# Reordering VectorE between neighbouring steps of an FFT convolution that shares one core with a gated MLP

## The chip, the cores and the metric

The kernel runs on one core of a Trainium2 chip. The metric is device time in microseconds (us) for one execution, and the time of a version is the median of its runs. The engines are named as in the profile: PE (TensorE), DVE (VectorE), ACT (ScalarE), POOL (GpSimd) and SP (SyncE, which here only issues transfers).

## The reference, cut to what matters

The input is normalised, goes through two branches, and the three are summed.

```python
def _A_ref(u, log_A_real, A_imag, C_real, C_imag, log_dt, D_skip):
    ...                                   # A, C from the parameters; P = exp(A dt pos)
    K = 2.0 * jnp.einsum("dn,dnl->dl", C, P).real       # D x L kernel, N = 256 terms
    Kf = jnp.fft.rfft(K, 2 * L)
    Uf = jnp.fft.rfft(u_t, 2 * L)
    y = jnp.fft.irfft(Uf * Kf[None, :, :], 2 * L)[:, :, :L]
    ...
    return y + u * D_skip[None, None, :]

def _B_ref(x, w_gate, w_up, w_down):
    h = _sigmoid(x @ w_gate) * (x @ w_up)
    return h @ w_down

xn = _layernorm(A_u)
return A_u + _A_ref(xn, ...) + _B_ref(xn, ...)
```

L = 2048 positions, D = 448 channels, N = 256 state terms, F = 1792 hidden units; everything is float32.

## The kernel before, in words

Two Python generators, `conv()` and `glu()`, write the instructions of the two branches. Each hands back an estimated cost at every `yield`; the loop at the end of the kernel always advances the one whose `done / total` is smaller. So the order in which the matmuls of both branches are written is a matter of these numbers alone: `total[0]` holds, among others, 17 times `WS` = 7.0 for the 17 steps described below. Tile then schedules the written instructions onto the engines' queues at build time: an instruction that is ready goes ahead of one that is not, a lower place in the text goes first, `hp(HP)` moves an instruction 300 places forward, and `tc.issue_after(x)` puts the instructions of a block behind x where both are on the same engine. On the chip every queue is worked through in that order.

**The MLP (`glu`).** It goes in two halves of 1024 tokens (two tiles of 512), and in each half over 14 slices f of 128 hidden units in groups of three (or two). For a slice and a token tile there are two *gate halves* of 11 matmuls each (gate and up projections, L710; float32 is made of a high and a low part, three products). ACT and DVE make `th`, `hf` (L721), `hh` and `hl` (L728) out of them. After a group come eight *down chunks* of 9 matmuls (6 in the group of two; L824), each added to `acc` by DVE (L829). In the second half the slices 4, 5, 0, 1 and 2 load raw weights through POOL's DMA queue and POOL itself splits them into high and low part (`wh` L772, `wl` L773, `dh` L798, `dl` L799); the raw gate/up weights and the raw down weights of these slices use one buffer, `wraw`, in turn. At the second chunk of the last group `glu` yields `None`: it is then held until `conv` is through.

**The convolution (`conv`).** A long part (`kgen`) generates K and its first transform stage until about 557 us. Then `spectra` makes the second stage of both transforms, the product, and the way back, in 17 *steps* (h, k): eight with h = 0 (channels 0 to 223), one for k = 32, eight with h = 1. The list `ks` gives the order of k. One step is:

- `there` (L892 to L926): 32 matmuls into the PSUM tile `pk` (from K) and 32 into `px` (from the input; L908). For each of the two, ACT copies the odd part to `oo` (L912), and DVE forms sum and difference of even part and `oo` (L914, L915), which are written to the tiles `kk` and `xx`. These four DVE instructions are called *the reading* (the "forward sums" of the change) here, since they free `pk` and `px`. Then come two products on DVE (`yy`, L919, and `kk` in place, L920), two combinations on POOL (L921 on `yy`; L922, which reads `kk` and writes `yy`), and DVE's *sum and difference* `sd` of the two halves of `yy` (L924, L925).
- `back` (L928 to L957): 32 matmuls of `sd` (L937) into the same two PSUM tiles `pk` and `px`, ACT's copies to `vt` (L943), and stores from `vt` to the DRAM tensor `v_d` (two transfers; six for k = 0).

`kk`, `xx` and `yy` have one buffer each, `sd` and `oo` two. The loop writes `there(n)`, then (after half a step's cost) `back(n-1)`, and so on. The input tiles of a step are loaded three steps ahead. PE's order is fixed: the list `sp_mm` holds the latest matmul and `issue_after` puts the next spectra block behind the MLP's matmuls that were written before it, and the other way round.

When two steps k and k+16 are through, `turned` loads their rows of `v_d` back as `vp` (SP's queue). When all of h = 0 is there, `last(0, q)` (L965 to L986) does the last stage for the quarters q = 0 to 3 of the positions: 64 matmuls (L973) into `pk` (even q) or `px` (odd q), which DVE adds to `ac` or `acc` (L982). In the loop two quarters are written together after one step, the other two together after the next. For h = 1, `last(1, q)` is written within the MLP's last group, after its fifth down chunk.

Of the kernel before, what the change touches and what calls it, by code (L numbers as in the profile page):

```python
# [15 lines left out]
ALU = mybir.AluOpType  # L16
# [12 lines left out]
NFT = F // 128  # L29
WK = 5.5  # L30
WS = 7.0
HOLE = 6
AHEAD = 46
WP = 5
WX = 2
HELD = 9
LATE = 3.6
HP = 300
Y0 = (8, 1)
# [13 lines left out]
NCK = D // DC  # L53
# [74 lines left out]
def s4d_glu_kernel(ctx, tc, io):  # L128
    nc = tc.nc
    hp = tc.high_priority  # L130
    v = nc.vector
# [106 lines left out]
    def out_end(src, b0, ds, engs=(nc.sync, nc.scalar)):  # L238
        for g in range(4):
            to = blocks(out_t, g, b0, src.shape[1])  # L240
            engs[g % len(engs)].dma_start(to[:, :, ds], src[32 * g : 32 * g + 32, :, ds])
# [606 lines left out]
    def spectra(pf):  # L848
# [16 lines left out]
        def work(n, sh, bufs):  # L865
            return spare[n].pop() if spare.get(n) else pf.tile(sh, F32, name=n, bufs=bufs)
# [22 lines left out]
        def after():  # L889
            return tc.issue_after(sp_mm[0].ins)  # L890

        def there(k, tb, sk, sx):  # L892

            n = 2 if k == 32 else 4
            np_ = 32 * n
            both = []
            for j, src in enumerate((sk, sx)):
                with after():
                    for c in range(2):
                        for g in range(n):  # L900
                            for p in range(2):
                                s = slice(64 * p, 64 * p + 64)
                                to = pb[j][32 * g : 32 * g + 32, p, H * c : H * c + H]
                                rhs = sx[s, g]
                                if src is sk:
                                    to, rhs = to.rearrange("p (g d) -> p g d", d=32), sk[s, :, g]
                                w = (t32[s, 0] if k == 32 else tb[s, g])[:, 32 * c : 32 * c + 32]
                                mm = nc.tensor.matmul(to, w, rhs, start=True, stop=True, skip_group_check=True)  # L908
                sp_mm[:] = [mm]
                ev, od = (half(pb[j][:np_, p, : 2 * H]) for p in range(2))  # L910
                oo = work("oo", [128, 2, H], 2)
                nc.scalar.copy(oo[:np_], od)  # L912
                t = work(("kk", "xx")[j], [128, 2, 2, H], 1)
                v.tensor_tensor(t[:np_, 0], ev, oo[:np_], ALU.add)  # L914
                v.tensor_tensor(t[:np_, 1], ev, oo[:np_], ALU.subtract)  # L915
                both.append(t[:np_])
            kk, xx = both
            yy = work("yy", [128, 2, 2, H], 1)[:np_]
            v.tensor_tensor(yy, kk, xx, ALU.mult)  # L919
            v.tensor_tensor(kk, kk, xx[:, :, ::-1], ALU.mult)  # L920
            nc.gpsimd.tensor_tensor(yy[:, :, 0], yy[:, :, 0], yy[:, :, 1], ALU.subtract)  # L921
            nc.gpsimd.tensor_tensor(yy[:, :, 1], kk[:, :, 0], kk[:, :, 1], ALU.add)  # L922
            sd = work("sd", [128, 2, 2, H], 2)
            v.tensor_tensor(sd[:np_, 0], yy[:, 0], yy[:, 1], ALU.add)  # L924
            v.tensor_tensor(sd[:np_, 1], yy[:, 0], yy[:, 1], ALU.subtract)  # L925
            return sd  # L926

        def back(h, k, sd, engs=(nc.sync, nc.sync)):  # L928
            vt = work("vt", [128, 4, H], 2)
            n = 2 if k == 32 else 4  # L930
            bt = t32[:, 1:].rearrange("p (q e) m -> p q e m", q=2) if k == 32 else bk
            with after():
                for e in range(2):
                    for g in range(n):
                        s = slice(32 * g, 32 * g + 32)
                        for p in range(2):
                            mm = nc.tensor.matmul(  # L937
                                pb[g // 2][64 * p : 64 * p + 64, g % 2, :H], bt[s, p, e], sd[s, p, e],
                                start=(e == 0), stop=(e == 1), skip_group_check=True,
                            )  # L940
            sp_mm[:] = [mm]
            for j in range(n // 2):
                nc.scalar.copy(vt[:, 2 * j : 2 * j + 2], pb[j][:, :, :H])  # L943

            for p in range(2):
                s = slice(64 * p, 64 * p + 64)
                real = slice(64 * p, 64 * p + 64, 2)
                to = lambda h_: v_d[h_, s].rearrange("(c g q) w d -> w c g q d", c=2, g=4)
                if k == 32:
                    for j in range(2):  # L950
                        engs[p].dma_start(to(j)[:, 1, 0, 0], vt[real, j])
                elif k == 0:
                    engs[p].dma_start(to(h)[:, 0, 0, 0], vt[real, 0])
                    for c in range(2):
                        engs[p].dma_start(to(h)[:, c, 1:, 0], vt[64 * p + c : 64 * p + 64 : 2, 1:])
                else:
                    engs[p].dma_start(to(h)[:, :, :, k // 4], vt[s])  # L957
# [7 lines left out]
        def last(h, q):  # L965

            for p in range(2):
                s = slice(64 * p, 64 * p + 64)
                for i in range(2):
                    for g in range(4):  # L970
                        w = 16 * (q % 2) + 4 * g + 2 * (q // 2) + i
                        with after():
                            mm = nc.tensor.matmul(  # L973
                                pb[q % 2][32 * g : 32 * g + 32, p, H * i : H * i + H], wf[s, w], vp[h][s, w],
                                start=True, stop=True, skip_group_check=True,
                            )
            sp_mm[:] = [mm]
            ds = slice(H * h, H * h + H)
            acc = ac[:, 4 * q : 4 * q + 4] if q < 2 else accs[q]
            for p in range(2):  # L980
                a = acc[:, p::2, ds]
                v.tensor_tensor(a, a, half(pb[q % 2][:, p, : 2 * H]), ALU.add)  # L982
            if h == 1 and q < 3:
                out_end(acc, 4 * q, ds, *([[nc.gpsimd]] if q == 0 else []))
            elif h == 0 and q < 2:
                out(acc, 4 * q, h)  # L986
# [2 lines left out]
        lasts.append(last)  # L989
        nc.sync.dma_start(t32, io["c_t32"])  # L990
        nc.gpsimd.dma_start(bk, io["c_bk"])
        ks = [4, 20, 0, 16, 8, 24, 12, 28]
        steps = [(0, k) for k in ks] + [(1, k) for k in ks[-NTB:] + ks[:-NTB]]
        steps[1:1] = [(None, 32)]
        tabs = {}
        ld = [loads(*s) for s in steps[:NLD]]
        nc.gpsimd.dma_start(wf, io["c_wf"])
        prev, wait, due = None, [], []
        for n, (h, k) in enumerate(steps):

            sp_mm[:] = glu_mm
            cur = there(k, *ld[n])
            if (h, k) == (0, ks[-NTB - 1]):
                for k_ in ks[:-NTB]:
                    tabs.pop(k_)
            if n + NLD < len(steps):
                ld.append(loads(*steps[n + NLD]))
            glu_on[:] = [1]
            yield WS / 2
            sp_mm[:] = glu_mm  # L1010
            if prev is not None:
                back(*prev)
            if 4 <= n < 8:
                o = slice(2 * n - 8, 2 * n - 6)
                nc.sync.dma_start(ac[:, o], acc_d[:, o])
            if prev is not None and prev[1] < 32:
                wait.append(prev[:2])

            while len(wait) > 2 and not (due and wait[0][0] == 1):
                t, u = wait.pop(0), wait.pop(0)  # L1020
                turned(*t, 4)
                if u == (0, 28):
                    due = [n + 1]
            prev = (h, k, cur)
            if n == 11:
                total[1] -= LATE
            yield WS / 2
            if due and n >= due[0]:
                sp_mm[:] = glu_mm
                for q in (0, 1, 2, 3)[2 * (n - due[0]) : 2 * (n - due[0]) + 2]:  # L1030
                    last(0, q)
                if n == due[0] + 1:
                    due = []
        sp_mm[:] = glu_mm
        back(*prev, (nc.sync, nc.scalar))
        for t in (*wait, prev[:2]):
            turned(*t)

    def conv():
# [87 lines left out]
        with tc.tile_pool(name="pf", bufs=1, side="right", reuse_waits="tile") as pf:  # L1127
            yield from spectra(pf)

    lasts, glu_mm, sp_mm, glu_on, outs, x1s, hfs, xls = [], [], [], [], [0], [0], [], []  # L1130
    xq, psc, raws, acl, marks, slots, pqs = list(x_first), [], [], [], [None, None], {}, []
    W1s, GGs, act = [], [], []
    gens = [conv(), glu()]
    total = [sum(Y0) + 11 * WP + 8 * WX + AHEAD + NCK * WK + HOLE + 17 * WS, 2 * (4 + NFT * 14.8) - HELD]
    done = [0.0, 0.0]
    done[0] += next(gens[0])
    held = False
# [38 lines left out]
```

## Time and profile before

| | |
|---|---|
| median of 3 runs | 762.92 us (757.61 to 768.84) |
| the profiled execution, its own time | 769.57 us |
| its span from first to last instruction | 767.8 us |
| mean granted TensorE clock in it | 0.945 |
| first `there` matmul of the 17 steps | 557.2 us |
| first `there` matmul of the last step | 726.0 us |

In the tables below a row of a timeline has start and duration in us, the engine, the line of the kernel, the operation with its output and inputs, how many instructions are merged into the row, and in square brackets how long the engine was idle before it and what it waited for. A row of the chain of waits has start, duration, engine, output and line. A row of the list of waits has total us, times and the longest. A row of the stage table has the stretch, its length, then busy us and instruction count of PE, PE's weight loads, DVE, ACT and POOL, the granted TensorE clock, the DMA share and GB/s. The times in the prediction are those of the profiled execution.

### The profile page before, as it was taken

The page shows a single profiled execution, that of the slowest core. Times are in us where ns is not written, and L with a number is a line of the kernel's source. Part 1 is how long each engine was busy: PE and PEld are TensorE (multiplying, and loading weights), DVE is VectorE, ACT ScalarE, POOL GpSimd, SP SyncE. Part 2 cuts the span into 40 slices and gives each one's busy share as a digit, 9 for nine tenths or more (in the row PEclk, how much of TensorE's full clock was granted, in tenths as well). Part 3 has the DMA queues.
Part 4 walks back from the last instruction along what each step waited for, and adds up shares of the span by engine and source line. Part 5 has one row for each costly group of instructions (what it writes and reads, how often), then busy time and mean ns, then how long its engine had stood idle before and what let it go on. Part 6 is the DMA issues. An engine that isn't in the chain of part 4 may idle for free.

```text
span 767.8 us, 22542 instructions
## 1 busy us (share of the span) xinstructions
PE 678.1 (88%) x9477; PEld 520.6 (68%) x9477; DVE 602.3 (78%) x777; ACT 423.1 (55%) x651; POOL 427.1 (56%) x455
## 2 busy tenths in 40 slices
PE   3897699999998988888899999899899799968966
PEld 2664588877876877555778777788667567645754
DVE  6798996789998998876659988787397567777843
ACT  3544466477787888787377777767413222212310
POOL 2110065748889889974636776754146553675211
PEclk9997989999999999798999999999999999988997
DMA  9934265345234543344744134304588757775464
GB/s 209 208 126 160 79 200 178 117 137 177 78 102 151 180 118 96 116 151 144 229 136 146 38 95 141 93 20 142 149 260 233 213 159 205 214 206 163 114 161 126
DMA packets 93462, 114.58 MB, mean 149 GB/s; under 512 B 12848, under 2 KB 83056, under 8 KB 93104
## 3 DMA queue, kind: packets, MB, share of 16 engines
q1 hardware_dynamic: 71632, 92.54, 41.1%
q10 hardware_dynamic: 19248, 14.91, 6.9%
q0 software_dynamic: 2480, 5.67, 2.8%
q8 instruction: 75, 1.23, 0.7%
q14 instruction: 27, 0.22, 0.1%
HBM read 68.32 MB, written 44.76 MB: 147 GB/s over the span
## 4 chain that ended last, share of the span: by engine, by line
PE 34%; DVE 9%; issue 4%; POOL 4%; DMA 4%; ACT 2%; SPq 1%; ACTq 0%; DVEq 0%; POOLq 0%
PE gu L710 14%; PE po L824 7%; PE ko L619 4%; PE tr L535 2%; POOL yy L921 1%; DMA v_d<-vt 1%; POOL yy L922 1%; PE pk L908 1%; DVE yy L919 1%; DVE Ft L605 1%; DVE sd L925 1%; PE kp L561 1%; PE px L908 1%; DMA wraw<-in_B_w_up_dram 1%; DMA rdw<-in_B_w_down_dram 1%
## 5 line engine op out<-in xcount | busy, mean ns | idle before, releaser
L513 POOL TENSOR_TENSOR me<-me,pm 128x32 f32<-128x32 f32 (+1 forms) x168 | 147.5, 878 | 84.3 <-DVE Et L604 69.6
L513 POOL TENSOR_TENSOR mf<-mf,pm 128x64 f32<-128x64 f32 (+1 forms) x112 | 122.7, 1095 | 6.1
L710 PE MATMUL gu<-xh,wh 128*128 128x512 f32 x336 | 107.8, 431 | 6.4 <-DVE acc L829 4.8
L710 PE MATMUL gu<-xh,wl 128*128 128x512 f32 x336 | 99.5, 404 | 0.0
L710 PE MATMUL gu<-xl,wh 128*128 128x512 f32 x336 | 98.3, 397 | 0.5 <-DVE xl L218 0.5
L824 PE MATMUL po<-dh,hh 128*128 128x448 f32 (+1 forms) x227 | 87.1, 384 | 10.0 <-DVE hf L721 3.8
L605 DVE TENSOR_TENSOR Ft<-mf,S 128x1024 f32<-128x1024 f32 x56 | 80.5, 1437 | 13.5 <-PE ko L619 4.4
L604 DVE TENSOR_TENSOR Et<-me,S 128x1024 f32<-128x1024 f32 x56 | 79.1, 1412 | 14.2 <-ACT me L526 14.2
L710 PEld LDWEIGHTS gu<-xh,wh 128*128 128x128 f32 x336 | 64.6, 203 | 30.2 <-issue 10.0
L824 PE MATMUL po<-dl,hh 128*128 128x448 f32 (+1 forms) x227 | 84.1, 370 | 0.0
L603 DVE TENSOR_TENSOR Et<-me,S 128x1024 f32<-128x1024 f32 x56 | 77.3, 1384 | 8.2 <-ACT S L546 7.9
L824 PE MATMUL po<-dh,hl 128*128 128x448 f32 (+1 forms) x227 | 82.8, 368 | 0.0
L543 ACT ACTIVATE S<-tr 128x1024 f32<-128x1024 f32 x56 | 57.7, 1031 | 43.6 <-PE tr L535 28.8
L726 ACT CAST hh<-hf 128x512 fp32r<-128x512 f32 x56 | 34.9, 623 | 78.3 <-DVE hf L721 77.7
L619 PEld LDWEIGHTS ko<-Et,Ft 128*32 128x32 f32 x3584 | 56.1, 115 | 30.3 <-DVE Ft L605 13.6
L710 PEld LDWEIGHTS gu<-xh,wl 128*128 128x128 f32 x336 | 66.0, 197 | 15.1
L619 PE MATMUL ko<-Et,Ft 128*32 128x64 f32 x3584 | 65.9, 228 | 11.5 <-DVE Ft L605 11.5
L710 PEld LDWEIGHTS gu<-xl,wh 128*128 128x128 f32 x336 | 63.7, 191 | 16.0 <-issue 1.4
L546 ACT ACTIVATE S<-S,hpi 128x1024 f32<-128x1024 f32 x56 | 65.6, 1171 | 0.0
L721 DVE SCALAR_TENSOR_TENSOR hf<-th,gu 128x512 f32<-128x512 f32 x56 | 38.1, 680 | 32.8 <-PE gu L710 26.1
L829 DVE SCALAR_TENSOR_TENSOR acc<-po,acc 128x448 f32<-128x448 f32 (+1 forms) x81 | 48.2, 608 | 18.6 <-PE po L824 18.6
L728 DVE TENSOR_TENSOR hl<-hf,hh 128x512 fp32r<-128x512 f32 x56 | 51.4, 918 | 14.3 <-ACT hh L726 14.2
(212 smaller groups left out, 1357.9 us busy)
## 6 DMA issues: line engine op xcount, KB each, us to landing
sk_d<-sk ACTq DMA_DIRECT2D x14, 512.0 KB
sx<-x_d SPq DMA_DIRECT2D x64, 112.0 KB
skl<-sk_d SPq DMA_DIRECT2D x16, 448.0 KB
vp<-v_d SPq DMA_DIRECT2D x7, 896.0 KB
v_d<-vt SPq DMA_DIRECT2D x27, 224.0 KB
wt_d<-wh SPq DMA_DIRECT2D x9, 512.0 KB
wt_d<-wl SPq DMA_DIRECT2D x9, 512.0 KB
wl<-wt_d SPq DMA_DIRECT2D x9, 512.0 KB
```

The source lines that it names most:

```text
L513: ins = nc.gpsimd.tensor_tensor(m[:, :, w + a : 2 * w : n], m[:, :, a:w:n], par(base + i).unsqueeze(2).to_broadcast([128, 4 * DC, w // n]) ...
L543: nc.scalar.activation(rows(cs), pv, AF.Abs)
L546: sins[:] = [nc.scalar.activation(cs, cs, AF.Sin, scale=-TWO_PI, bias=hpi)]
L603: v.tensor_tensor(Et[:, :, :, 32:64], two(me[:, :, 32:64]), S[:, 1::-1], ALU.mult)
L604: v.tensor_tensor(Et[:, :, :, 0:32], two(me[:, :, 0:32]), S[:, 1:3, :, ::-1], ALU.mult)
L605: fts[:] = [v.tensor_tensor(Ft, two(mf), S[:, 3:5], ALU.mult)]
L619: nc.tensor.matmul(ko[32 * j : 32 * j + 32, sl], Ft[:, cc, DC * h + 4 * q + j], Et[:, cc, DC * h + 4 * q + j], start=(k == 0), stop=(k == ...
L710: glu_mm[:] = [nc.tensor.matmul(ps, a_, b_, start=(n == 0), stop=(n == len(mm) - 1))]
L721: marks[1] = v.scalar_tensor_tensor(hf, th, 1.0, pgu[1], ALU.add, ALU.mult)
L728: v.tensor_tensor(hl, hf, hh, ALU.subtract)
L824: glu_mm[:] = [nc.tensor.matmul(po[:, ds], a_[:, bs], w_[:, ds], start=(n == 0), stop=(n == 3 * fc - 1))]
L829: v.scalar_tensor_tensor(acc[:, b, ds], po[:, ds], 0.5, acc[:, b, ds], ALU.mult, ALU.add)
```

## The change

It has four edits.

1. `there` is cut in three. It now ends with the reading and returns `kk`, `xx` and the reading's last instruction. The products and POOL's combinations become `product`, where POOL's two instructions get `hp(HP)`. The sum and difference become `halves`. The loop writes `there(n)`, then `halves` of step n-1 behind the reading of step n, then `product` of step n. So DVE's order changes from reading n, products n, sd n, reading n+1 to reading n, sd n-1, products n, reading n+1, sd n.
2. In the loop the quarters of `last(0, q)` are no longer written in pairs: after each one `conv` yields half a step's cost, so that MLP matmuls stand behind each quarter.
3. `total[0]` counts 19 instead of 17 times `WS`, for these four half steps.
4. The order of k goes from 4, 20, 0, 16, 8, 24, 12, 28 to 4, 20, 8, 24, 0, 16, 12, 28; the second half of the channels, which begins with the last four, goes from 8, 24, 12, 28, 4, 20, 0, 16 to 0, 16, 12, 28, 4, 20, 8, 24.

```diff
                 v.tensor_tensor(t[:np_, 0], ev, oo[:np_], ALU.add)
-                v.tensor_tensor(t[:np_, 1], ev, oo[:np_], ALU.subtract)
+                read = v.tensor_tensor(t[:np_, 1], ev, oo[:np_], ALU.subtract)
                 both.append(t[:np_])
-            kk, xx = both
+            return *both, read
+
+        def product(np_, kk, xx):
             yy = work("yy", [128, 2, 2, H], 1)[:np_]
             v.tensor_tensor(yy, kk, xx, ALU.mult)
             v.tensor_tensor(kk, kk, xx[:, :, ::-1], ALU.mult)
-            nc.gpsimd.tensor_tensor(yy[:, :, 0], yy[:, :, 0], yy[:, :, 1], ALU.subtract)
-            nc.gpsimd.tensor_tensor(yy[:, :, 1], kk[:, :, 0], kk[:, :, 1], ALU.add)
+            with hp(HP):
+                nc.gpsimd.tensor_tensor(yy[:, :, 0], yy[:, :, 0], yy[:, :, 1], ALU.subtract)
+                nc.gpsimd.tensor_tensor(yy[:, :, 1], kk[:, :, 0], kk[:, :, 1], ALU.add)
+            return yy
+
+        def halves(np_, yy):
             sd = work("sd", [128, 2, 2, H], 2)
...
-        ks = [4, 20, 0, 16, 8, 24, 12, 28]
+        ks = [4, 20, 8, 24, 0, 16, 12, 28]
...
-            cur = there(k, *ld[n])
+            np_ = 64 if k == 32 else 128
+            kk, xx, read = there(k, *ld[n])
+            if prev is not None:
+                with tc.issue_after(read.ins):
+                    sd = halves(*prev[2:])
+            cur = np_, product(np_, kk, xx)
...
-                back(*prev)
+                back(*prev[:2], sd)
...
                 for q in (0, 1, 2, 3)[2 * (n - due[0]) : 2 * (n - due[0]) + 2]:
+                    sp_mm[:] = glu_mm
                     last(0, q)
+                    yield WS / 2
...
-        back(*prev, (nc.sync, nc.scalar))
+        back(*prev[:2], halves(*prev[2:]), (nc.sync, nc.scalar))
...
-    total = [sum(Y0) + 11 * WP + 8 * WX + AHEAD + NCK * WK + HOLE + 17 * WS, 2 * (4 + NFT * 14.8) - HELD]
+    total = [sum(Y0) + 11 * WP + 8 * WX + AHEAD + NCK * WK + HOLE + 19 * WS, 2 * (4 + NFT * 14.8) - HELD]
```

More of the change, by code (lines that the diff above doesn't have):

```diff
@@ L1023, in spectra @@
                     due = [n + 1]
-            prev = (h, k, cur)
+            prev = (h, k, *cur)
             if n == 11:
```

## The prediction, made before the changed kernel was run

> **What bounds the kernel now.** I read the stage table first, to see where PE is not full; then who waits for whom; then one step on DVE and POOL; then the chain of waits.
>
> ```profile
> 300.00:540.00 240.00, 223.60 (x3846) 172.53 (x3841) 189.29 (x203) 175.39 (x260) 157.84 (x182) 0.95 0.39 121
> 557.00:709.00 152.00, 132.18 (x1709) 94.21 (x1708) 112.08 (x153) 37.19 (x71) 86.94 (x78) 0.92 0.74 208
> 709.00:731.00 22.00, 22.00 (x338) 15.65 (x344) 18.69 (x27) 7.97 (x15) 5.44 (x5) 1.00 0.47 127
> ```
>
> Ahead of the steps PE is busy 223.6 of 240 us. In the first 13 steps it stands still for 152 - 132.2 = 19.8 us at a granted clock of 0.92; in the last steps it is full. So PE's work sets the time, and what can be won lies in PE's waits and in its clock between 557 and 709 us. The list of PE's waits from 556 us on names them:
>
> ```profile
> PE pk L937 <- DVE kk L915: 9.9, 6, 3.0
> PE pk L973 <- DMA vp<-v_d: 5.7, 1, 5.7
> PE pk L908 <- DVE ac L982: 5.2, 1, 5.2
> PE pk L908 <- DVE acc L982: 3.3, 1, 3.3
> PE pk L937 <- DVE sd L924: 2.3, 1, 2.3
> PE pk L937 <- issue: 0.8, 1, 0.8
> ```
>
> Six times `back` waits for the reading that frees `pk`, twice `there` for the adds of a pair of quarters. Why the reading is late is seen in one step on DVE, and beside it on POOL:
>
> ```profile
> 622.07 0.62 DVE L924 TENSOR_TENSOR sd<-yy 128x448 f32<-128x448 f32 x1 [2.75 <-POOL yy L922]
> 622.62 0.62 DVE L925 TENSOR_TENSOR sd<-yy 128x448 f32<-128x448 f32 x1
> ...
> 624.52 0.69 DVE L728 TENSOR_TENSOR hl<-hf,hh 128x512 fp32r<-128x512 f32 x1 [0.69 <-ACT hh L726]
> 625.13 0.62 DVE L914 TENSOR_TENSOR kk<-pk,oo 128x448 f32<-128x448 f32 x1
> ...
> 626.72 0.61 DVE L915 TENSOR_TENSOR xx<-px,oo 128x448 f32<-128x448 f32 x1
> 627.37 1.09 DVE L919 TENSOR_TENSOR yy<-kk,xx 128x896 f32<-128x896 f32 x1
> 628.50 1.09 DVE L920 TENSOR_TENSOR kk<-kk,xx 128x896 f32<-128x896 f32 x1
> ...
> 631.87 0.62 DVE L924 TENSOR_TENSOR sd<-yy 128x448 f32<-128x448 f32 x1 [2.28 <-POOL yy L922]
> ```
>
> ```profile
> 628.61 2.00 POOL L921 TENSOR_TENSOR yy<-yy 128x448 f32<-128x448 f32 x1 [6.57 <-DVE yy L919]
> 630.69 1.15 POOL L922 TENSOR_TENSOR yy<-kk 128x448 f32<-128x448 f32 x1
> ```
>
> It is a ring through DVE and POOL, 631.87 - 622.07 = 9.8 us a turn: `sd`, the MLP's `hf` and `hl`, the reading, the products, POOL's two, `sd` again. What PE needs for a step stands in the chain of waits:
>
> ```profile
> 554.83 2.43 PE po L824 x12
> ...
> 569.51 0.99 PE pk L937 x16
> ...
> 570.62 1.10 PE px L937 x16
> 571.72 4.16 PE gu L710 x11
> ...
> 583.91 0.92 PE pk L908 x32
> 584.83 0.76 PE px L908 x32
> 585.59 2.78 PE gu L710 x11
> ```
>
> ```profile
> 683.33 1.75 PE pk L908 x32
> 685.08 1.49 PE px L908 x32
> 686.57 3.14 PE gu L710 x11
> ...
> 690.76 2.71 PE gu L710 x11
> ...
> 698.69 1.75 PE pk L908 x32
> 700.44 1.49 PE px L908 x32
> 701.94 3.94 PE gu L710 x11
> ```
>
> At full clock `there` takes 585.59 - 583.91 = 1.68, a gate half 2.7 (690.76), a matmul of a down chunk 2.43 / 12 = 0.20, and a `back` whose matmuls alternate between the banks 690.76 - (686.57 + 3.14) = 1.05. So a step with two gate halves needs 1.68 + 5.4 + 1.05, about 8.2 us on PE; where the ring takes 9.8, PE waits.
>
> **The change part by part: what goes.** (a) With the reading ahead of `sd`, `back(n-1)` no longer waits for it behind POOL: 9.9 + 0.8 = 10.7 us.
>
> (b) After each quarter MLP matmuls now stand on PE (a gate half of 2.7 or a down chunk of 9 x 0.20 = 1.8), and they cover the adds: two per quarter, of the size of L914, 0.62. These adds no longer stand behind an `sd` that waits for POOL. 5.2 + 3.3 = 8.5 us. If the cover were gone, half of it would be back.
>
> (c) After a wait PE runs slower for a while:
>
> ```profile
> 602.45 1.65 PE L710 MATMUL gu<-xh,wh 128*128 128x512 f32 x3
> 616.30 1.65 PE L710 MATMUL gu<-xh,wh 128*128 128x512 f32 x3
> 628.40 0.96 PE L710 MATMUL gu<-xh,wh 128*128 128x512 f32 x3
> ```
>
> Three matmuls in 1.65 instead of 0.96, and a whole gate half in 4.16 (571.72) instead of 2.7. Three such gate halves cost 3 x 1.4 = 4.2; the two `there` at 683.33 and 698.69 took 3.24 instead of 1.68 and the gate halves behind them 0.4 and 1.2 more, together 4.7. In all 8.9 us, if no long wait is left. [...]
>
> (d) In the chain the `back` at 569.51 does 16 matmuls on `pk` and then 16 on `px`, 571.72 - 569.51 = 2.2 us instead of 1.05: it was put in that order because the reading frees `pk` first. The six that waited for L915 I take to be the same. After the change `sd` comes last and frees both banks' work at once, so they should alternate. 7 x 1.1 = 7.7; I take 6, ends 0 and 7.7.
>
> Together 10.7 + 8.5 + 8.9 + 6 = 34.1 us.
>
> **What is added.** (e) `back(n-1)` now needs the reading of n and then `sd` of n-1. From the rows of DVE that is 626.72 + 0.61 - 625.13 = 2.2 and 622.62 + 0.62 - 622.07 = 1.2, so 3.4 us after `there(n)`. What PE has in between follows from the costs of the yields, walked through `done / total`; for the kernel before, that walk gives the order the trace shows. In ten steps it is one gate half: wait 3.4 - 2.7 = 0.7, ten times 7.0. In two it is one down chunk of 1.8: 1.6 each, 3.2. In step 1 a chunk of six matmuls, 1.2: wait 2.2. In the others two chunks, no wait. Sum 12.4. The low end is 0.1 a step, when the first matmuls start on the first half of `sd` (0.6 sooner); the high end 1.1, when `hl` stands ahead of the reading. Queued behind the waiting `back` are MLP matmuls and, behind them, `there(n+1)`; on DVE the products stand behind `sd`, so a late POOL delays them, not the reading of `xx`.
>
> [...]
>
> (f) In the last step `sd` of step 15 now stands between the reading and the products that lead to the end: +1.2. The six stores of k = 0 leave the last steps; the final store in the chain has company there:
>
> ```profile
> 739.29 5.86 DMA v_d<-vt
> ```
>
> I take nothing for it; the ends are 0 and 2 us of gain. In the middle, where k = 0 goes, no PE wait of the list is for a transfer of a step.
>
> (g) With 19 instead of 17 times 7.0 the convolution's total goes from 559 to 573. At the first step its `done` is 440, so the MLP, total 413, stands at 0.768 instead of 0.787 of it: 8 units less, by the walk two gate halves and two chunks of six, 2 x 2.7 + 2 x 1.2 = 7.8 us of PE work that moves from ahead of the steps into them. Ahead PE is 93% busy (223.6 / 240), so the steps begin earlier by most of it. I take a loss of 1.8; ends 0 and 7.8.
>
> (h) POOL's two go ahead of weight splits: 1 us, see the second rival.
>
> Sum: 34.1 - 12.4 - 1.2 - 1.8 - 1 = 17.7 us. The profiled execution took 769.57, so 751.9, a ratio of 0.977; that execution was 0.9% above the median, and 0.977 of 762.92 is **745 us**. With the ends of (d), (e) and (g) this case has a range of 737 to 754.
>
> **The rivals.** *The reading cannot go ahead* (the change does not do what it says): `kk` has one buffer, and L922 reads it, so the reading's first instruction must wait for POOL whatever its place. Then the ring is hardly shorter and only (b) with its 4.7 of (c) is won: 13.2, less 4 x 0.7 in the steps where PE is full now and 1.2 at the end, 9.2; 0.988 of the median, 754 us. For it: the row of L922. Against it: without `hf` and `hl` the ring is 2.2 + 1.2 + 1.1 + (630.69 + 1.15 - 628.61 = 3.2), 7.7, below PE's 8.2, so POOL is through when the reading starts. It decides if `hf` and `hl` (1.9 from 622.62 + 0.62 to 625.13) stay in the ring.
>
> *The weights of the last slices come late.*
>
> ```profile
> 672.42 2.68 POOL L773 TENSOR_TENSOR wl<-wraw,wh 128x1024 fp32r<-128x1024 f32 x1
> 694.21 2.35 POOL L773 TENSOR_TENSOR wl<-wraw,wh 128x1024 fp32r<-128x1024 f32 x1
> ```
>
> POOL delivers slices 1 and 2 at 675.1 and 696.6, 21.5 us apart. Slice 1 is first used at 686.57, 11.5 us later. With (b) and the gate halves between the quarters PE goes from slice 1 to slice 2 in 4 gate halves, 2 `there`, 2 `back` and 2 waits, about 18 us. The slack of over 11 us shrinks by what is gained before and by these 3.5; if it is used up, up to 5 us are lost: 750.
>
> *The clock does not recover*, since short waits of 0.7 remain in most steps: (c) is lost, 8.9 us, 754. For it: the slow gate half after 0.8 us; against it: 628.40, at full speed.
>
> *Slower*: POOL's second instruction comes late in most steps, the reading, `sd` and `back` all queue behind it, and PE's clock drops each time. It decides when the mean wait of `back` passes 2 us, against 3.0 for the longest now. At 2.0 and 1.4 for the gate half behind it, 16 steps cost 54 instead of 12.4: 745 + 42 = 787. Against it: POOL is idle 6.57 us ahead of L921 in the step shown.
>
> **How the numbers follow.** Chances: forecast 0.60, the reading held 0.18, weights 0.10, clock 0.05, slower 0.07. Two per cent, about what a measurement of this kernel can tell from no change, is 747.7. The forecast lies below it in about 0.63 of its cases, weights and held reading in a few: faster 0.45, within 0.48, slower 0.07. For eight in ten: 735 to 761.
>
> **What would show it.** On DVE the four reading instructions directly followed by `sd` without a wait for L922; no PE wait for L982 in the loop; PE waits of L937 for `sd` instead of L915, about 0.7 each; alternating L937; clock near 1.0 from 557 to 709; first `there` at about 551. Wrong: L914 waiting for L922, PE waiting for weights at L710, or a clock still near 0.92.

## The result, and the profile after

The changed kernel takes 757.78 us (median of 20 runs, 752.06 to 765.21) against 762.8 us (median of 20 runs, 756.32 to 771.21) for the kernel before on the same chip: a ratio of 0.994, 95% interval 0.992 to 0.997. The forecast was 745 us, a ratio of 0.977. The sign was right, the size was not: some 5 us came of 17.7.

The profiled execution of the changed kernel took 761.07 us, with a span of 759.3. Its stage table, with the columns explained above:

```profile
557.00:709.00 152.00, 132.78 (x1755) 94.49 (x1747) 107.59 (x158) 39.21 (x76) 84.64 (x79) 0.95 0.73 209
709.00:731.00 22.00, 19.09 (x245) 13.27 (x243) 16.72 (x22) 6.66 (x13) 7.10 (x6) 0.99 0.40 107
```

PE is busy 132.8 of the same 152 us, where it was 132.2: as many holes as before. Its list of waits says which (total us, times, longest):

```profile
PE pk L943 <- DVE sd L930: 18.0, 13, 6.7
PE pk L943 <- issue: 3.5, 1, 3.5
...
PE pk L979 <- DMA out_dram<-acc: 0.8, 1, 0.8
PE pk L943 <- ACT th L718: 0.7, 1, 0.7
PE pk L979 <- ACT vt L949: 0.6, 1, 0.6
PE pk L979 <- DVE ac L988: 0.4, 1, 0.4
```

The old waits in the loop are gone: none of `back` for the reading (it was L915), none of `there` for the adds (L982 before, L988 now). What stands there instead is one kind of wait, that of `back` for `sd`. It had been forecast at 12.4 us in the loop. It is 18.0 + 3.5, less the 3.2 of the last `back`, which lies in the tail: 18.3.

Another part of what is missing lies in the old time. The profiled execution of before that the prediction was worked from was one of its slowest, 769.57 us in runs that go up to 771.21. A second profile of the unchanged kernel took 761.41 us (span 759.6), and its list of waits and its stage row read:

```profile
PE pk L937 <- DVE kk L915: 5.4, 3, 3.3
PE pk L973 <- DMA vp<-v_d: 5.1, 1, 5.1
PE pk L908 <- DVE ac L982: 5.1, 1, 5.1
PE pk L908 <- DVE acc L982: 3.7, 1, 3.7
...
PE pk L937 <- issue: 1.2, 1, 1.2
```

```profile
557.00:709.00 152.00, 135.09 (x1770) 96.92 (x1758) 117.99 (x162) 39.49 (x77) 85.44 (x78) 0.96 0.77 216
```

Of the 10.7 us of waits for the reading only 6.6 are there, and the clock is 0.96 instead of 0.92. Set against this execution, the changed one differs like this, from the starts of the `there` blocks in the two timelines:

| | before, second profile | after | difference |
|---|---|---|---|
| first `there` | 555.5 | 549.3 | -6.2 |
| from there to the last `there` | 163.3 | 171.0 | +7.7 |
| from there to the end | 40.8 | 39.0 | -1.8 |
| span | 759.6 | 759.3 | -0.3 |

The middle stretch holds 23 more matmuls of L710 and 11 more of L824 (276 against 253, 120 against 109). At 2.7 / 11 and at 0.20 us each these are 5.6 + 2.2 = 7.8 us of MLP that were moved into it, as forecast. So, apart from the moved work, the stretch from the first `there` to the last takes as long as before: 163.2 against 163.3.

Two places show what went wrong. In the first, a step goes as planned up to `sd`. DVE and then POOL, by their timelines:

```profile
617.93 0.61 DVE L914 TENSOR_TENSOR kk<-pk,oo 128x448 f32<-128x448 f32 x1
...
619.53 0.61 DVE L915 TENSOR_TENSOR xx<-px,oo 128x448 f32<-128x448 f32 x1
620.06 2.13 DVE L930 TENSOR_TENSOR sd<-yy 128x448 f32<-128x448 f32 x1
622.11 0.61 DVE L931 TENSOR_TENSOR sd<-yy 128x448 f32<-128x448 f32 x1
```

```profile
619.34 2.36 POOL L773 TENSOR_TENSOR wl<-wraw,wh 128x1024 fp32r<-128x1024 f32 x1
```

The reading is directly followed by `sd`, as the change wants it. But `sd` takes 2.13 us instead of 0.61: it began 0.7 us after POOL's weight split and ended at 622.19, 0.5 us after the split's end at 621.70. L915, begun beside the same split, took 0.61. In this execution five instructions of `sd` began beside a split (L773 or L799) and took 0.70, 1.11, 1.51, 2.01 and 2.13 us, each ending 0.5 us after it; ten of the reading, which take one operand from a PSUM tile, did so and took 0.60 or 0.61. No term of the sum stands for this. PE waits 2.05 us here, and the matmuls behind that wait are slow, at a granted clock of 0.60 (last section).

The second place is the costliest. POOL's timeline, then DVE's, then PE's:

```profile
690.47 0.78 POOL L645 DMA_DIRECT2D wraw<-in_B_w_gate_dram  x1 [0.29 <-POOL dl L799]
...
693.05 1.04 POOL L647 DMA_DIRECT2D wraw<-in_B_w_up_dram  x2
696.42 1.04 POOL L772 CAST wh<-wraw 128x1024 fp32r<-128x1024 f32 x1 [2.33 <-DMA wraw<-in_B_w_up_dram]
697.54 2.38 POOL L773 TENSOR_TENSOR wl<-wraw,wh 128x1024 fp32r<-128x1024 f32 x1
699.90 1.12 POOL L924 TENSOR_TENSOR yy<-yy 128x448 f32<-128x448 f32 x1
...
701.57 1.14 POOL L925 TENSOR_TENSOR yy<-kk 128x448 f32<-128x448 f32 x1
```

```profile
702.74 0.62 DVE L914 TENSOR_TENSOR kk<-pk,oo 128x448 f32<-128x448 f32 x1 [8.35 <-POOL yy L925]
```

```profile
706.13 0.60 PE L943 MATMUL pk<-sd,bk 32*64 32x224 f32 x1 [6.71 <-DVE sd L930]
```

The products of this step were ready at 694.4 (the second one started at 693.31 and took 1.08). The first sum began at 699.90, since POOL's queue held six issues of transfers, a wait of 2.33 us for one of them, a cast and a split ahead of it. The next reading needs `kk`, which has one buffer and is read by the second sum, so DVE stood for 8.35 us and PE for 6.71. This is the rival "the reading cannot go ahead", in a step in which POOL is late. DVE's list of waits has L914 waiting for L925 four times, 11.6 us in all.

### The profile page after: what moved, and what is told of

It reads as the page before. It is cut to its first block, busy times and chain, and to the rows that moved or that the text cites. A ratio compares the mean times of both kernels' runs of the same rounds, so it can differ in the third digit from the quotient of the medians.

```text
span 759.3 us, 22540 instructions
## 1 busy us (share of the span) xinstructions
PE 672.3 (89%) x9477; PEld 516.2 (68%) x9477; DVE 604.2 (80%) x777; ACT 421.7 (56%) x651; POOL 438.4 (58%) x455
## 4 chain that ended last, share of the span: by engine, by line
PE 46%; DVE 25%; DMA 8%; POOL 6%; issue 6%; ACT 6%; SPq 2%; DVEq 0%; ACTq 0%; POOLq 0%
PE gu L710 21%; PE po L824 9%; PE ko L619 6%; PE tr L535 3%; DVE Et L604 3%; DVE Ft L605 3%; DVE Et L603 2%; PE pk L943 2%; DVE acc L829 2%; POOL me L513 2%; DMA wraw<-in_B_w_up_dram 2%; DVE hl L728 1%; DVE hf L721 1%; DMA xe<-in_A_u_dram 1%; DVE pm L449 1%
## 5 line engine op out<-in xcount | busy, mean ns | idle before, releaser
L513 POOL TENSOR_TENSOR me<-me,pm 128x32 f32<-128x32 f32 (+1 forms) x168 | 163.4, 972 | 63.7 <-DVE Et L604 48.7
L710 PE MATMUL gu<-xh,wh 128*128 128x512 f32 x336 | 107.5, 429 | 9.3 <-DVE acc L829 4.8
L710 PE MATMUL gu<-xh,wl 128*128 128x512 f32 x336 | 97.9, 399 | 0.0
L710 PE MATMUL gu<-xl,wh 128*128 128x512 f32 x336 | 96.9, 395 | 0.0
L824 PE MATMUL po<-dh,hh 128*128 128x448 f32 (+1 forms) x227 | 89.3, 394 | 6.6 <-DVE hf L721 2.9
L604 DVE TENSOR_TENSOR Et<-me,S 128x1024 f32<-128x1024 f32 x56 | 82.4, 1471 | 8.2 <-ACT me L526 5.9
L603 DVE TENSOR_TENSOR Et<-me,S 128x1024 f32<-128x1024 f32 x56 | 78.7, 1407 | 12.8 <-ACT S L546 12.7
L710 PEld LDWEIGHTS gu<-xh,wh 128*128 128x128 f32 x336 | 63.0, 200 | 34.1 <-issue 10.8
L824 PE MATMUL po<-dl,hh 128*128 128x448 f32 (+1 forms) x227 | 85.9, 378 | 0.0
L824 PE MATMUL po<-dh,hl 128*128 128x448 f32 (+1 forms) x227 | 84.7, 377 | 0.0
L710 PEld LDWEIGHTS gu<-xh,wl 128*128 128x128 f32 x336 | 64.9, 193 | 14.8
L710 PEld LDWEIGHTS gu<-xl,wh 128*128 128x128 f32 x336 | 64.0, 191 | 15.3 <-issue 1.4
L924 POOL TENSOR_TENSOR yy<-yy 128x448 f32<-128x448 f32 (+1 forms) x17 | 29.7, 1744 | 70.8 <-DVE yy L921 69.4
L829 DVE SCALAR_TENSOR_TENSOR acc<-po,acc 128x448 f32<-128x448 f32 (+1 forms) x81 | 48.1, 608 | 22.2 <-PE po L824 22.1
```

Source lines behind the costliest of these rows:

```text
L513: ins = nc.gpsimd.tensor_tensor(m[:, :, w + a : 2 * w : n], m[:, :, a:w:n], par(base + i).unsqueeze(2).to_broadcast([128, 4 * DC, w // n]) ...
L603: v.tensor_tensor(Et[:, :, :, 32:64], two(me[:, :, 32:64]), S[:, 1::-1], ALU.mult)
L604: v.tensor_tensor(Et[:, :, :, 0:32], two(me[:, :, 0:32]), S[:, 1:3, :, ::-1], ALU.mult)
L710: glu_mm[:] = [nc.tensor.matmul(ps, a_, b_, start=(n == 0), stop=(n == len(mm) - 1))]
L824: glu_mm[:] = [nc.tensor.matmul(po[:, ds], a_[:, bs], w_[:, ds], start=(n == 0), stop=(n == 3 * fc - 1))]
L829: v.scalar_tensor_tensor(acc[:, b, ds], po[:, ds], 0.5, acc[:, b, ds], ALU.mult, ALU.add)
```

## The experiments

The second profile of the kernel before, shown above, was the first of the runs.

> The kernel before, unchanged, for a second profile of it. If the recorded profile of before was an ordinary one, the first there starts again at about 557 us and the span is about 768 us. If its front part was slow by accident, the first there starts about 4 to 5 us earlier and the rest is alike; the comparison of stages with the changed kernel then has to use this one.

It was neither. The first `there` came 1.7 us earlier (555.5 against 557.2), and the stretch behind it was 6.5 us shorter (204.1 against 210.6). So most of what sets the two profiles apart lies in the steps and behind them.

All ratios are against the kernel before on the same chip. Which parts of the change they have, and what was measured:

| run | sums on | reading | last stage | ratio (95%) | median us | waits of `back`, us | first `there` to end, us |
|---|---|---|---|---|---|---|---|
| before (second profile) | POOL | old | pairs | 1 | 761.41 (one run) | 9.6 | 204.1 |
| e1 | POOL | ahead | pairs | 0.997 (0.993 to 1.002) | 762.32 | 20.7 | 204.2 |
| e2 | POOL | old | quarters | 1.008 (1.005 to 1.011) | 768.23 | 17.7 | 220.1 |
| after | POOL | ahead | quarters | 0.994 (0.992 to 0.997) | 757.78 | 22.2 | 210.0 |
| e8 | VectorE | old | pairs | 0.980 (0.974 to 0.986) | 746.83 | 4.5 | 189.6 |
| e11 | VectorE | ahead | pairs | 0.989 (0.980 to 0.997) | 751.70 | 13.3 | 195.7 |
| e10 | VectorE | old | quarters | 0.980 (0.971 to 0.988) | 746.85 | 7.6 | 198.2 |
| e5 | VectorE | ahead | quarters | 0.983 (0.978 to 0.988) | 751.23 | 13.1 | 200.1 |

The last two columns are of the one profiled execution of each; the waits are those of the `back` matmuls in PE's list, the tail's too. The medians come from several chips and are not to be compared with each other; the ratios are. Quarters go with 19 times WS, pairs with 17, so by the count above the stretch of a kernel with quarters holds 7.8 us more of MLP. e1, e10, e11, e5 and after have the new order of k, e2 and e8 the old.

**e1: the reading ahead and the new order of k, the quarters in pairs again.**

```diff
-                    sp_mm[:] = glu_mm
                     last(0, q)
-                    yield WS / 2
-    total = [... + 19 * WS, ...]
+    total = [... + 17 * WS, ...]
```

> The changed kernel with the last stage's quarters in pairs again and 17 times WS, so edits 1 and 4 alone. Theory A (putting the reading ahead gains nothing: PE's waits for the reading, 10.7 us before, only become waits for the sum and difference, 18 us after; all of the gain is that of the quarters): ratio to before 1.000 to 1.010, with the two waits of there for the adds, 8.5 us, back. Theory B (the reading ahead is worth what was forecast for it, and the quarters are what disappoints): ratio 0.985 to 0.993.

No change that can be measured: 0.997, between the two theories. The new wait of `back` is there as in the changed kernel (16.6 + 2.1 + 2.0 us). The wait for the adds has nearly gone though the quarters stand in pairs: one wait of 0.4 us of `there` for L988 is left of 8.8. In the second profile of before, an `sd` that had waited 2.80 us for POOL and took 1.53 stood right ahead of the adds of the first pair (675.64); in e1 no `sd` stands between the products and these adds (674.13). So the new order on VectorE is enough to end this wait, and the MLP matmuls between the quarters are not needed for it.

**e2: the quarters alone, in the kernel before.** The same four lines the other way round, in the old code.

> The kernel before with edits 2 and 3 alone (a yield behind each quarter, 19 times WS). Theory A: the 8.5 us of waits and 4.7 us of slow clock behind them go, ratio 0.980 to 0.988, faster than the whole change. Theory B: 0.995 to 1.000, no faster than the whole change.

Slower, 1.008, and outside both theories. The waits for the adds fall to 2.0 + 1.5 us, but those of `back` rise to 17.7. Its longest are 4.66 (step 1, `sd` beside a split), 4.15 (POOL's sums behind the weights, as in the second place above) and 3.60. What stands at the last, on DVE, POOL and PE:

```profile
598.23 2.82 DVE L925 TENSOR_TENSOR sd<-yy 128x448 f32<-128x448 f32 x1
...
602.93 0.62 DVE L914 TENSOR_TENSOR kk<-pk,oo 128x448 f32<-128x448 f32 x1
```

```profile
597.90 2.66 POOL L773 TENSOR_TENSOR wl<-wraw,wh 128x1024 fp32r<-128x1024 f32 x1
```

```profile
604.23 1.40 PE L937 MATMUL pk<-sd,bk 32*64 32x224 f32 x12 [3.60 <-DVE kk L915]
```

It is the same collision of `sd` with a weight split, in the old order with the reading queued behind. The steps that meet a split are others than in the profiles of before. By e1 and e2 neither half of the change gains what was forecast. Together they are clearly better (0.994) than the quarters alone; that they are better than the reading alone isn't shown, since e1's interval reaches down to 0.993.

**e5: POOL's two sums of a step on VectorE, in the changed kernel.**

```diff
-            with hp(HP):
-                nc.gpsimd.tensor_tensor(yy[:, :, 0], yy[:, :, 0], yy[:, :, 1], ALU.subtract)
-                nc.gpsimd.tensor_tensor(yy[:, :, 1], kk[:, :, 0], kk[:, :, 1], ALU.add)
+            v.tensor_tensor(yy[:, :, 0], yy[:, :, 0], yy[:, :, 1], ALU.subtract)
+            v.tensor_tensor(yy[:, :, 1], kk[:, :, 0], kk[:, :, 1], ALU.add)
```

> The changed kernel with the two combinations of a step (yy) on VectorE instead of GpSimd. Theory C (what is lost is lost to POOL: the combinations queue behind weight transfers and splits, the sum and difference meets a split, and PE's clock drops behind these waits): PE's waits for the sum and difference fall from 18 us to under 9 and the ratio to before is 0.975 to 0.987. Theory D (the way from there over the reading and the sum and difference is too long by itself, and VectorE is as full as it may be): two more instructions of about 0.6 us a step make the waits longer, ratio 0.995 to 1.010.

0.983, as theory C had it. With POOL's sums off the step the change comes near to its forecast, though VectorE is now busy for 130.0 us of the stage instead of 107.6 (the stage also holds more matmuls, 1920 against 1755). Stage row and the waits of `back`:

```profile
557.00:709.00 152.00, 141.70 (x1920) 100.85 (x1920) 130.04 (x195) 42.28 (x81) 43.29 (x48) 0.97 0.75 210
```

```profile
PE pk L942 <- DVE sd L929: 9.4, 10, 2.5
PE pk L942 <- issue: 3.7, 1, 3.7
```

So, by the two ratios, some 1.1% had been lost by the way over POOL. Of the waits that are left, 9.4 + 3.7 us, the last `back` has 2.1; the 11.0 in the loop are near the 12.4 that the prediction had for it.

**e8: the same two lines on VectorE, in the kernel before.** Nothing else is changed.

> Before, with POOL's two sums on VectorE and nothing else changed: the old order of reading, the quarters in pairs. Theory R0 (the old order is bad only because the sums come from POOL): the reading then stands behind VectorE's own work alone, some 8.9 us a step, PE's wait for the reading falls from 9.9 to under 2 us, the waits for the adds stay, ratio 0.983 to 0.990. Theory R (the reading's place matters by itself, since it stands behind the sums, `sd`, `hf` and `hl`): at least half of the waits for the reading stay, 0.993 to 1.0; then only the two together give the 0.983 that the sums on VectorE gave in the changed kernel.

0.980: the fastest, together with e10, and without any part of the change. Stage row and waits:

```profile
557.00:709.00 152.00, 144.78 (x2017) 104.38 (x2016) 139.81 (x208) 44.77 (x87) 45.33 (x50) 0.98 0.80 223
```

```profile
PE pk L908 <- DVE ac L982: 2.7, 1, 2.7
PE pk L937 <- issue: 1.8, 1, 1.8
PE pk L937 <- DVE sd L924: 1.6, 1, 1.6
...
PE pk L937 <- DVE kk L915: 0.3, 1, 0.3
```

The wait for the reading is 0.3 + 1.8 us, and that for the adds fell from 8.8 to 3.1 (2.7, and 0.4 for the second pair) by itself, which neither theory had. So most of what was bad in the old order came from `sd`, which stood on VectorE ahead of the reading and waited there for POOL. Once `sd` is ready when its turn comes, `back(n-1)` has its `sd` long before and waits for the reading alone. A rival would be that the collisions with the weight splits had gone too. They had not: in e8 one of the two sums, now on VectorE, took 2.82 us instead of 0.62 (592.12, beside a split begun at 591.33).

**e10 and e11: the other two corners.** e10 is e8 with edits 2 to 4; e11 is e5 with the pairs and 17 times WS.

> The reading in its old place, the last stage by quarters and the new order of k, and the two sums on VectorE instead of POOL: the kernel with the sums on VectorE (0.983) with the reading alone put back. Theory N (once POOL is out of the ring, the new place of the reading only costs: `back` then waits for the reading and for `sd`, 3.4 us against a gate half of 2.7, and its matmuls take 1.38 instead of 1.05): waits of `back` under 3 us instead of 9.4 + 3.7, steps of 8.1 to 8.7 us instead of 9.1, ratio to before 0.968 to 0.978. Theory M (the new place is worth something by itself, and the old order without POOL was good for another reason): 0.983 or more.

> The changed kernel with the sums on VectorE (0.983) and the last stage by pairs again with 17 times WS: the reading ahead and the order of k, without the quarters. Against it stands the kernel before with the sums on VectorE (0.980), which differs in the reading's place and the order of k alone. Theory N: slower than that one by the new waits of `back`, 9 to 13 us less the one or two that its adds still cost: 0.985 to 0.997. Theory M: as fast or faster, 0.970 to 0.981.

e10 gives 0.980, between the two theories, and e11 0.989, as theory N had it. Both intervals are wide. The waits of `back` are told apart more clearly, first e10's, then e11's:

```profile
PE pk L937 <- issue: 3.5, 1, 3.5
...
PE pk L937 <- DVE kk L915: 2.5, 2, 1.3
...
PE pk L937 <- DVE sd L924: 1.6, 1, 1.6
```

```profile
PE pk L942 <- DVE sd L929: 9.2, 7, 2.6
PE pk L942 <- issue: 2.1, 1, 2.1
PE pk L942 <- DVE sd L930: 2.0, 1, 2.0
```

With POOL's sums on VectorE the new place of the reading has more waits, by 5.5 us with the quarters and 8.8 with the pairs. In time the two corners with the old place are the faster ones, by 0.4% and 0.8%, but the intervals overlap: that the new place costs time there is likely and not shown. A gain of it is not to be seen there. (The order of k differs between e8 and e11 as well.)

**e7 and e13: the weights off POOL, the sums left there.** In e7 the casts and splits of the late weights are made on ScalarE and VectorE; in e13 their transfers go to SP's queue as well.

```diff
-                            nc.gpsimd.tensor_copy(wh, raw)
-                            nc.gpsimd.tensor_tensor(wl, raw, wh, ALU.subtract)
+                            nc.scalar.copy(wh, raw)
+                            v.tensor_tensor(wl, raw, wh, ALU.subtract)
```

> After, but the splits of the weights that come late (wh, wl, dh, dl of the slices that are read again) are made on ScalarE (the two casts) and VectorE (the two subtractions); POOL keeps the two sums of each step and its transfers. Theory C1 (POOL's weight work is what takes the gain: it stands ahead of the sums in POOL's queue, and it blocks `sd` at SBUF): nearly as good as with the sums on VectorE, ratio to before 0.983 to 0.988; the wait of `back` for `sd` at most 11 us instead of 18.0, the reading's wait for POOL's second sum under 3 us instead of 11.6, no `sd` over 1 us. Theory C2 (the way over POOL is too long in itself, 3.2 us and two handovers, with or without the weights): as after, 0.991 to 0.997, the waits hardly less.

0.997, as theory C2 had it, and the waits of `back` for `sd` didn't fall (19.3 us). The time of `sd` itself did: with no split on POOL, 18 of its rows between 557.22 and 676.47 have 0.61 or 0.62 us. But the run doesn't single out the handover: the reading's waits for POOL did fall, from 11.6 us to 7.0, and at the longest of them six issues of transfers still stood ahead of the sums in POOL's queue, 3.6 us of them. POOL, then DVE:

```profile
600.27 0.76 POOL L645 DMA_DIRECT2D wraw<-in_B_w_gate_dram  x1 [6.22 <-DVE dl L799]
...
603.89 1.39 POOL L924 TENSOR_TENSOR yy<-yy 128x448 f32<-128x448 f32 x1
```

```profile
606.53 0.62 DVE L914 TENSOR_TENSOR kk<-pk,oo 128x448 f32<-128x448 f32 x1 [2.24 <-POOL yy L925]
```

> As the kernel with the weight splits on ScalarE and VectorE (0.997), and the transfers of those weights on SP's queue: of the steps POOL has nothing left but the two sums. In that kernel POOL issued six transfers (3.6 us) ahead of the sums of a step, and the reading waited 2.2 us for them. Theory C1' (POOL's queue is what delays the sums, its transfers too): no wait of the reading for POOL over 0.5 us, the step of 15.6 us falls to 9 to 11, ratio 0.984 to 0.992, unless SP's queue, which now holds transfers that wait for a buffer, delays a step's own loads. Theory C2 (the handover itself): the waits for POOL stay at 7 us or more, 0.992 to 1.0.

1.011, slower than before, and outside both theories. e7's step of 15.6 us did fall to 10.4, and the reading waited for POOL no longer than 1.3 us at a time; but five such waits made 5.8 us, so a part of the loss is the way over POOL itself. The time went elsewhere, to VectorE's splits, which now stand in its queue and wait, by way of ScalarE's casts, for a transfer. ACT, then DVE:

```profile
677.27 1.05 ACT L772 CAST wh<-wraw 128x1024 fp32r<-128x1024 f32 x1 [6.61 <-DMA wraw<-in_B_w_up_dram]
```

```profile
678.35 1.23 DVE L773 TENSOR_TENSOR wl<-wraw,wh 128x1024 fp32r<-128x1024 f32 x1 [5.43 <-ACT wh L772]
682.81 0.63 DVE L799 TENSOR_TENSOR dl<-rdw,dh 128x448 fp32r<-128x448 f32 x1 [3.23 <-ACT dh L798]
```

`back` waited 8.34 us behind these two. The pair of runs therefore can't say how much of POOL's share is its weight work and how much the handover. It shows that work that waits for a transfer was dear in both queues that the step goes through.

**e15: only the first of the two sums on VectorE**, in the changed kernel.

> The changed kernel with the first of POOL's two sums on VectorE: POOL's own part of a step falls from about 3 us to 1.15, VectorE's grows by 0.7, and the second sum stays in POOL's queue behind its transfers and weight splits. Theory C1 (the queue): the wait of 8.35 us of the reading for POOL in the step from 694.9 to 711.5 stays within 2 us of its size, and the time stays near the changed kernel's: ratio to before 0.990 to 0.995. Theory C2 (the length of the way over POOL): most waits go, 0.981 to 0.988, near the kernel with both sums on VectorE (0.983).

0.984 (0.978 to 0.990), and the long wait is still there, in the step with the weight split:

```profile
694.45 0.63 DVE L914 TENSOR_TENSOR kk<-pk,oo 128x448 f32<-128x448 f32 x1 [6.49 <-POOL yy L925]
```

C1 was right on the wait and C2 on the time. Taking the first sum from POOL brings most of what e5 brings in the ratio, by the middle of a wide interval. Both mechanisms are in it, and their shares stay open.

**e3: POOL's sums without priority**, and **e6: the old order of k**, both in the changed kernel.

> After, with POOL's two sums planned without priority: only POOL's queue has another order. Theory C1: in the steps in which a weight slice is split (five slices, splits of 2.5 and 1.1 us) the sums fall behind the splits, 2 to 3 us in each of two to five steps: ratio to before 0.998 to 1.010, longer waits of the reading for POOL's second sum. Theory C2: the order of the queue is not what counts, 0.992 to 0.996. My sum had 1 us for this edit.

> After, with the old order of the steps (k = 0 and its six stores late again). If the order of k gave what the end of the kernel gained (the stretch from the last `there` to the end is 39.0 us in after, 40.9 in the second profile of before), that stretch is 40 to 41 us and the ratio to before 0.996 to 0.999; everything ahead of it stays as in after. If it gave nothing: 0.992 to 0.996 and 39 us.

e3: 0.992 (0.989 to 0.995), no worse than the changed kernel; the reading waited 8.57 us for POOL in the same step. The priority doesn't put the sums ahead of the weights in the step that counts. e6: 0.994 (0.991 to 0.997), with 40.0 us from the last `there` to the end instead of 39.0. The order of k is worth nothing that can be measured in the time.

A second buffer for `kk`, which would free the reading from POOL's second sum, wasn't tried. So the single buffer's share in the loss is argued from the waits and not shown by a run.

## Why the prediction was wrong, point by point

**What bounds the kernel** was read rightly: the ring over DVE and POOL. e8 takes POOL's two sums out of it and changes nothing else, and 2% go.

**(a), 10.7 us: over-sized.** The waits went as forecast, but they were 6.6 us in the second profile of the same kernel. They differ between executions, and the one used was among the slowest.

**(b), 8.5 us: right**, 8.8 in the second profile, all gone. Of its two reasons the second, the adds no longer behind a waiting `sd`, is enough for all but 0.4 us (e1).

**(c), 8.9 us: failed.** The step was "if no long wait is left". Long waits are left, 2.05, 3.46 and 6.71 us, and the clock of the stage is 0.95 against 0.96 in the second profile. What PE's waits, `back` and the moved work don't account for is some 2.4 us, which is all that the clock can have given: the waits in the loop rose from 16.1 us (5.4 + 5.1 + 3.7 + 1.2 + 0.7) to 19.6 (18.3 + 0.7 + 0.6), `back` fell by 1.2, and the steps stayed the same.

**(d), 6 us: wrong.** Its step was "`sd` comes last and frees both banks' work at once, so they should alternate". The banks do alternate, but the two halves of `sd` don't come at once. The first matmul starts as soon as the first half (L930) is there; that the matmuls on the second half follow as a group is inferred from this, since the rows don't show which half a matmul reads. A `back` that waited for `sd` takes 1.38 us at a granted clock of 1.00: in the step below the MLP's next matmul starts at 584.88.

```profile
583.50 0.37 PE L943 MATMUL pk<-sd,bk 32*64 32x224 f32 x1 [0.25 <-DVE sd L930]
```

It is less than the 2.0 of the grouped banks and more than the 1.05 of the last steps before. Behind the waits of 3.46 and 6.71 it is 2.2 and 2.15, at a granted clock of 0.50. Over 17 steps `back` takes 24.2 us against 25.4: 1.2 gained.

**(e), 12.4 us: the step that failed, and that (c) hangs on.** It measured 18.3, 5.9 more. "Wait 3.4 - 2.7 = 0.7" holds roughly where POOL isn't much in the way: those waits are 0.17 to 1.10, together 6.0 against the 8.8 that they were given. Three steps have the rest: 2.05 where `sd` stood behind a split, 6.71 where the sums stood behind the weights, and 3.46 instead of 2.2 in step 1, where again a split ran beside `sd`, which took 2.01. Against the 0.7, 0.7 and 2.2 they were given, these are 1.35 + 6.0 + 1.26 = 8.6 us too much. For the collision with a split the sum had no term. The sentence "a late POOL delays them, not the reading of `xx`" was wrong where it mattered: a late POOL delays the reading of `kk`, one step on, and with it that of `xx`, which stands behind it.

**(f), (g), (h).** The tail gained 1.8 us where 1.2 of loss was forecast. Nearly all of it lies in the last stage (from its first L973 or L979 to the next L824), which took 4.4 us behind a wait of 0.8 instead of 6.1 behind one of 5.1 for `vp`; the sum had nothing for it. e6 has the same 4.4 with the old order of k, so that order isn't the cause. Why `vp` came in time stays open. (g) came out right in this pair of executions: work of 7.8 us moved, start 6.2 earlier, 1.6 lost against 1.8 forecast; but the 1.8 had been a choice between 0 and 7.8, so that it is so near is partly luck. (h) is nothing that can be measured (e3).

So in this pair of executions 16.1 us of waits, some 2.4 of clock and 1.2 of `back` are removed, 19.6 of waits and 1.6 by (g) added, and 1.8 gained in the tail: -0.3 us, the difference of the spans (the 2.4 of clock is what was left over, so the sum is a statement of sizes and no proof). Against the forecast (c) falls short by 6.5 us, (e) costs 5.9 more, and (d) and (a) fall short by 4.8 and 4.1. The upper bound of 754 was narrower than its own terms as well: the far ends of (d), of (g) and, in ten steps, of (e) would add 6 + 6 + 4 = 16 us to 745. The medians are 5 us apart, so these two executions are not the typical pair; what the terms are in a typical pair wasn't measured.

**The rivals.** "The reading cannot go ahead" came true in four steps instead of all, and cost much in one of them (8.35 of 11.6 us). "The clock does not recover" came true in its outcome and not by its mechanism: behind the short waits of the loop (up to 1.10) the changed kernel's gate halves ran at full speed (a granted clock of 1.00, 613.03 to 615.77 behind the 1.10), and what was slow stood behind the three long ones (0.53 from 565.05 to 569.67, 0.60 from 623.71 to 628.00, 0.50 from 706.13 to 708.28). In "the weights come late" PE never waited for weights, but the weights' way through POOL did set the time from 690 to 702. The "slower" rival had the right mechanism for the longest wait, POOL's second sum late, with the reading, `sd` and `back` queued behind. It was held against it that POOL is idle for 6.57 us ahead of a sum in the one step shown; the step that counts was another. One step stood for all 17 there.

## What to carry to other kernels

When a step waits on another engine's result, follow that engine's queue through every step, with the transfers it issues and what these wait for, not through one good step. Moving the waiting instruction later traded one wait for another here, while two instructions moved to the engine that needs their result gave 2% in the old order, more than the whole reordering. And size a removed wait from two executions at least.

## What the runs showed of the hardware that was not expected

The clock after a short wait. PE in the changed kernel, after waits of 1.10 and of 2.05 us of `back`, with the first three matmuls of the gate half behind each:

```profile
611.66 0.37 PE L943 MATMUL pk<-sd,bk 32*64 32x224 f32 x1 [1.10 <-DVE sd L930]
...
613.03 0.97 PE L710 MATMUL gu<-xh,wh 128*128 128x512 f32 x3
...
622.33 0.37 PE L943 MATMUL pk<-sd,bk 32*64 32x224 f32 x1 [2.05 <-DVE sd L930]
...
623.71 1.38 PE L710 MATMUL gu<-xh,wh 128*128 128x512 f32 x3
```

After 1.10 us of waiting they run at full speed, after 2.05 they take 1.38 and the next three of one kind 1.48 instead of 0.85. The granted clock was 1.00 from 613.03 to 615.77 and 0.60 from 623.71 to 628.00; through the wait of 2.05 and the `back` behind it, it was still 1.00.

The length of the wait alone doesn't decide. In the first profile of before, the gate halves behind waits of 0.84 and 1.26 us ran at a granted clock of 0.63 (571.72 to 575.81, 602.45 to 606.58), and the one behind 1.61 us at 1.00 (628.40 to 631.12). What does decide stays open.

Six issues of transfers on POOL took 3.6 us of its time (600.27 to 603.89 in e7), more than the two sums of a step in the prediction's rows (3.2). And 32 matmuls of `back`, the same in number and shape, took 1.05, 1.38 or 1.98 us at a granted clock of 1.00 (714.98 in the second profile of before, 583.50 in the changed kernel, 626.42 in the first profile). The first go between the banks in fours and the last take 16 on `pk` and then 16 on `px`; the second go between the banks too, and what makes them slower than the first isn't shown.
